# Front of a fused attention and gated-FFN kernel: eight value channels mixed without a copy, copies dealt out anew, and the first query products moved ahead of the mixing weights

## The chip, the cores and the metric

The kernel runs on one core of a Trainium2 chip. The time is the device time of one execution in microseconds (us), the median of several runs. Names used below: PE is TensorE's matrix products, PEld its weight loads, DVE is VectorE, ACT is ScalarE, POOL is GpSimd, SP is SyncE. PSUM is the memory that TensorE writes and that VectorE and ScalarE copy from.

## The reference, cut to what matters

Four batches, eight heads, a sequence of 768, head size 64, eight blocks of 96 positions. An 8 x 8 matrix `P` per batch and head is normalised five times by rows and columns, and mixes the blocks of k and v. Each block of q then attends to its mixed block, and the result goes through a gated FFN (512 to 1536 to 512).

```python
for _ in range(5):
    P = np.exp(P - np.max(P, axis=-1, keepdims=True))
    P = P / (np.sum(P, axis=-1, keepdims=True) + 1e-09)
    P = P / (np.sum(P, axis=-2, keepdims=True) + 1e-09)
k_sorted = np.einsum('bhij,bhjcd->bhicd', P, k_b)
v_sorted = np.einsum('bhij,bhjcd->bhicd', P, v_b)
scores = scale * np.matmul(q_b, k_sb.transpose(0, 1, 2, 4, 3))
attn = softmax(scores)                       # shortened
x = np.matmul(attn, v_sb)                    # heads put side by side: 3072 x 512
out = (silu(x @ w_gate) * (x @ w_val)) @ w_out
```

## The kernel before, in words

The order on each engine is written out by hand (`manual_schedule`): all engines for the front part (batch 0 up to the first FFN products), TensorE and GpSimd after it. The change is in the front.

**Loads.** GpSimd issues the loads in order: v of batch 0 in two halves of 48 positions (`load_v`), the first half of q (`load_q0(0)`), k of batch 0 in two halves, and, behind its own copies, the gate and value weights (`load_gv`), the second half of q, v of batch 1 and so on. A natural v tile `v_tiles[0]` has 64 partitions (head and block) by positions by 64 channels.

**Copies of v.** Mixing v needs, for each channel, the 96 positions side by side. `copy_v` writes v from position-major into `vch`, which is channel-major (64 channels of 96 positions). Before the change it is dealt out by positions: GpSimd copies positions 0 to 24 and 72 to 96, and channels 40 to 64 of positions 60 to 72 (lines 150 to 152); ScalarE copies 24 to 36 after the exponential of iteration 2, 36 to 48 after that of iteration 3 (lines 201 to 204), and 48 to 72 less GpSimd's part after the loop (lines 218, 219).

**Normalisation.** Five iterations go to and fro between ScalarE (exponential, line 196) and VectorE (lines 206 to 212), with a small result `p_bf` (line 215). Meanwhile TensorE runs products whose result nothing reads: `dots(124)`, then a few 512-column ones (`fill`) behind each iteration's row sums (lines 454 to 458).

**Mixing weights.** `weights(0)` and `weights(1)` (line 464) spread `p_bf` over the two halves of the partitions into the bank `w_ps`; `mix_rows` (line 469, VectorE) masks it into the mixing matrix `rmix[0]`, whose low rows serve v and both halves serve k.

**Chunks.** `v_chunk(b, at, n, eng, tag)` makes the mixed v of n channels, one product for each (line 276, tile `tv`): the channel's 96 positions (and 32 columns beyond, which are not read later) are the weights, 128 columns wide, and `rmix` is what is streamed. Then `drain` copies the chunk out of PSUM into `vt`, on VectorE ("v", line 223) or ScalarE ("s", line 225). `k0_chunk` (line 265, tile `tk`) and `q0_chunk` (line 255, tile `tq`) do the same for k and q into `kqt`, two products for each position. The tag names the PSUM room: "a" and "b" are one tile of two banks each, "gen" is three single banks in turn, "x" is one bank. A chunk of 16 takes "a" or "b", smaller ones a "gen" bank. The normalisation's `p_ps`, `w_ps` and the v and k chunks share "gen"; `w_ps` is read until the mixing matrices of batches 1 to 3 are made, after the chunks.

**The order on TensorE at the end of the front** (lines 472 to 490) is

```python
weights(0); weights(1)
mix_rows(low); mix_rows(high)
q0_chunk(0, 0, 16, "s", "b")
v_chunk(0, 0, 8, "v", "gen"); v_chunk(0, 8, 8, "s", "gen"); v_chunk(0, 16, 16, "v", "a")
v_chunk(0, 32, 8, "v", "gen"); v_chunk(0, 40, 16, "s", "b"); v_chunk(0, 56, 8, "s", "gen")
k0_chunk(0, 16, "v", "a"); k0_chunk(16, 16, "s", "b"); k0_chunk(32, 8, "v", "gen"); k0_chunk(40, 8, "s", "gen")
q0_chunk(0, 16, 8, "v", "a")
fill(idle_ps, 4)
qk(0, 0, "a"); qk(0, 1, "b")
```

(calls put on fewer lines, arguments of `mix_rows` shortened). `qk` are the first score products (line 308), which need all of `kqt`. After the scores, the products with v (`av`, line 335) and the transposes follow the FFN's products (lines 386, 404, 421), in which the attention of the later batches is spread out.

Of the kernel before, what the change touches and what calls it, by code (L numbers as in the profile page):

```python
# [10 lines left out]
BF16 = mybir.dt.bfloat16  # L11
# [6 lines left out]
def kernel(  # L18
# [11 lines left out]
    nc = tc.nc  # L30

    B, H, S, D = q.shape
    NB = sort_net.shape[-1]
    C = S // NB
# [21 lines left out]
    vnp = ctx.enter_context(tc.tile_pool(name="vnp", bufs=1))  # L56
# [18 lines left out]
    vch = const.tile([128, D * C + 32], BF16)  # L75
# [8 lines left out]
    v_tiles = {}  # L84
# [18 lines left out]

    def load_v(b, lo, hi):
        if b // 2 not in v_tiles:
            v_tiles[b // 2] = vnp.tile([128, C, D], BF16, name=f"v{b // 2}", tag="vn")
        u = b % 2
        nc.gpsimd.dma_start(out=v_tiles[b // 2][u * R:(u + 1) * R, lo:hi], in_=v_nat[b, :, lo:hi, :])

# [3 lines left out]
    def load_gv(lo, hi):  # L113
        load_w(wg_sb, wg_dram, lo, hi)
        load_w(wv_sb, wv_dram, lo, hi)

    def copy_v(eng, pair, rows, s, n=4, d0=0, d1=D):
        cs = slice(s * (C // n), (s + 1) * (C // n))
        dst = vch3[rows, d0:d1, cs]
        src = v_tiles[pair][rows, cs, d0:d1]  # L120
        if eng is nc.scalar:
            eng.copy(dst, src.transpose([0, 2, 1]))  # L122
        else:
            eng.tensor_copy(dst, src.transpose([0, 2, 1]))  # L124
# [8 lines left out]
    HC = C // 2  # L133
# [7 lines left out]
    def load_q0(t):  # L141
        nc.gpsimd.dma_start(out=q0[t].rearrange("p c d -> p (c d)"), in_=q_runs[0, t])

    load_v(0, 0, HC)
    load_v(0, HC, C)
    make_identity(nc, ident)
    load_q0(0)
    for a, rows in enumerate(halves):
        nc.gpsimd.dma_start(out=k0[rows], in_=k_nat[0, :, a * HC:(a + 1) * HC, :])
    copy_v(nc.gpsimd, 0, lowr, 0)  # L150
    copy_v(nc.gpsimd, 0, lowr, 3)
    copy_v(nc.gpsimd, 0, lowr, 5, 8, 40, D)
    load_gv(0, 512)
    load_q0(1)
    load_gv(512, 1024)
    load_gv(1024, DF)
    load_v(1, 0, HC)
    load_v(1, HC, C)
    for lo, hi in ((0, 64), (64, C)):
# [35 lines left out]
    for it in range(N_ITER):  # L195
        nc.scalar.activation(p_ps, p_sb if it == 0 else p_ps, AF.Exp)
        if it == 1:
            with nc.allow_low_precision("0/1 mask"):
                nc.vector.tensor_reduce(mask, id4, axis=AX.XY, op=ALU.add)
            nc.scalar.copy(sel, ident.rearrange("p (r g two) -> p two g r", g=H2, two=2))  # L200
        if it == 2:
            copy_v(nc.scalar, 0, lowr, 2, 8)
        if it == 3:
            copy_v(nc.scalar, 0, lowr, 3, 8)
        rowred = rowreds[it]
        nc.vector.reduce_sum(rowred[:, :, 0], p_ps, axis=AX.X)
        nc.vector.reciprocal(rowred, rowred)
        nc.vector.tensor_mul(p_ps, p_ps, rowred.to_broadcast([BH, NB, NB]))
        nc.vector.reduce_sum(colred[:, 0, :], p_ps.transpose([0, 2, 1]), axis=AX.X)
        nc.vector.reciprocal(colred, colred)  # L210
        if it < N_ITER - 1:
            nc.vector.tensor_mul(p_ps, p_ps, colred.to_broadcast([BH, NB, NB]))
    for lo in (0, NB // 2):
# [1 line left out]
        nc.vector.tensor_tensor(  # L215
            p_bf[:, part], p_ps[:, part].unsqueeze(2).to_broadcast([BH, NB // 2, H, NB]),
            colred.unsqueeze(1).to_broadcast([BH, NB // 2, H, NB]), op=ALU.mult)
    copy_v(nc.scalar, 0, lowr, 4, 8)
    copy_v(nc.scalar, 0, lowr, 5, 8, 0, 40)

    def drain(eng, dst, src):
        if eng == "v":
# [13 lines left out]
    def chunk_tile(name, n, tag):  # L236
        return pair_tile(name, tag) if n == 2 else bank_tile(name, tag)
# [12 lines left out]
    def q0_chunk(t, at, n, eng, tag):  # L250
        dst = kqt_tile(0)[:, GI * C:2 * GI * C].rearrange("p (g t r c) -> p t g r c", g=H2, t=2, c=QC)[:, t]
        tp = chunk_tile("tq0", n // 8, tag).rearrange("p (l g r) -> p l g r", l=n, g=H2)
        for lc in range(n):
            for two in range(2):
                nc.tensor.matmul(tp[two * D:(two + 1) * D, lc], lhsT=q0[t][:, at + lc, :],
                                 rhs=sel[:, two], start=True, stop=True)
        drain(eng, dst[:, :, :, at:at + n], tp.rearrange("p l g r -> p g r l"))

    def k0_chunk(at, n, eng, tag):
        dst = kqt_tile(0)[:, 0:GI * C].rearrange("p (n a c) -> p a n c", a=2, c=HC)  # L260
        rm = rmix[0].rearrange("p a (g two) i -> p two a g i", two=2)
        tp = chunk_tile("tk0", n // 8, tag).rearrange("p (l a n) -> p l a n", l=n, a=2)
        for lc in range(n):
            for two in range(2):
                nc.tensor.matmul(tp[two * D:(two + 1) * D, lc].rearrange("p a (g i) -> p a g i", g=H2),
                                 lhsT=k0[:, at + lc, :], rhs=rm[:, two], start=True, stop=True)
        drain(eng, dst[:, :, :, at:at + n], tp.rearrange("p l a n -> p a n l"))

    def v_chunk(b, at, n, eng, tag):
        rows = slice(0, 128) if b % 2 else lowr  # L270
        dst = vt_tile(b // 2)[:, b % 2]
        mix = rmix[b][rows, 0].rearrange("p a b -> p (a b)")
        tp = chunk_tile("tv", n // 8, tag).rearrange("p (l n) -> p l n", n=H * NB)
        for ld in range(n):
            col = (at + ld) * C
            nc.tensor.matmul(tp[:, ld, :], lhsT=vch[rows, col:col + 128], rhs=mix,  # L276
                             start=True, stop=True)
        drain(eng, dst[:, :, at:at + n], tp[0:C].transpose([0, 2, 1]))

    def v_pair_chunk(pair, at, n, eng, tag):  # L280
# [168 lines left out]
    def dots(n):  # L449
        for _ in range(n):  # L450
            nc.tensor.matmul(idle_ps[0:32, 0:32], lhsT=warm_sb[:, 0:32], rhs=warm_sb[:, 0:32],
                             start=True, stop=True)

    dots(124)
    for it, n in ((1, 3), (2, 4), (3, 4), (4, 4)):
        nc.tensor.matmul(idle_ps[0:NB, 0:NB], lhsT=rowreds[it][:, :, 0], rhs=rowreds[it][:, :, 0],
                         start=True, stop=True)
# [4 lines left out]
    def weights(half):  # L462
        for i in range(NB):
            nc.tensor.matmul(w_ps[halves[half], i].rearrange("p b h -> p (b h)"),
                             lhsT=p_bf[:, i].rearrange("p a b -> p (a b)"),
                             rhs=ident[0:BH, 0:BH], start=True, stop=True)

    def mix_rows(dst, rows, b):
        nc.vector.tensor_tensor(dst, mask[rows].unsqueeze(2).to_broadcast([R, H, NB]),
                                w_ps[rows, :, b].transpose([0, 2, 1]), op=ALU.mult)  # L470

    weights(0)
    weights(1)
    mix_rows(rmix[0][lowr, 0], lowr, 0)
    mix_rows(rmix[0][highr, 1], highr, 0)
    q0_chunk(0, 0, 16, "s", "b")
    v_chunk(0, 0, 8, "v", "gen")
    v_chunk(0, 8, 8, "s", "gen")
    v_chunk(0, 16, 16, "v", "a")
    v_chunk(0, 32, 8, "v", "gen")  # L480
# [1 line left out]
    v_chunk(0, 56, 8, "s", "gen")  # L482
    k0_chunk(0, 16, "v", "a")
    k0_chunk(16, 16, "s", "b")
    k0_chunk(32, 8, "v", "gen")
    k0_chunk(40, 8, "s", "gen")
    q0_chunk(0, 16, 8, "v", "a")
    fill(idle_ps, 4)
# [105 lines left out]
        return todo  # L594

    for s in range(4):
        copy_v(nc.gpsimd, 0, highr, s)
    load_k_pair()
    load_v(2, 0, C)
    load_v(3, 0, C)  # L600
# [8 lines left out]
    merge(ffn(1), kqs(1, (4.6, 5.9, 10.4)) + vs(v_chunk, 16, (7.2, 7.9, 8.5, 9.1))  # L609
          + units(1, range(4), (11.7, 16.4), (3.1, 2.4)))  # L610
    for s in range(4):
        copy_v(nc.gpsimd, 1, both, s)
    nc.vector.memset(kqt_tile("p")[:, 2 * GI * C:], 0.0)
    merge(ffn(2), units(1, range(4, 8), (0.0, 5.5)) + kqs("p", (13.0, 14.7, 20.7)) + v_pairs([(0, 22.5)])
          + [(13.0, lambda: q_dma(2)), (16.4, lambda: q_dma(3))])
# [40 lines left out]
```

## Time and profile before

| what | value |
|---|---|
| time before, median of 3 runs | 248.41 us (248.22 to 248.43) |
| the profiled execution's own time | 248.79 us |
| its span, first to last instruction | 246.7 us |
| PE busy | 236.6 us, 96% of the span |
| PEld, DVE, ACT, POOL busy | 140.3, 157.7, 109.8, 50.3 us |
| granted TensorE clock | 1.0 throughout |
| first value product (`tv`) | 12.65 us after the span's start |
| first score product (`qk`) | 18.41 us |
| first FFN product (`g_ps`) | 23.16 us |
| products of the FFN (lines 386, 404, 421), busy | 76.6, 77.3, 62.1 us |

Times in the views are microseconds from the span's start. Busy times of matrix products overlap one another, since they are pipelined; what counts for TensorE is the distance from start to start. The chain that ended last goes back from the last instruction to whatever released it, step by step: a line of it is a piece of the time.

### The profile page before, as it was taken

To read this page: it belongs to the slowest core of one execution; us is meant where nothing else is said; L and a number is where in the kernel's file an instruction comes from. 1 tells how busy PE (TensorE), PEld (TensorE's weight loads), DVE (VectorE), ACT (ScalarE), POOL (GpSimd) and SP (SyncE) were. 2 spreads that over 40 slices of the span, in tenths; PEclk is the share of its full clock that TensorE was granted. 3 is DMA by queue.
4 is the path that set the end of the run, shared out by engine and by line. 5 is a ranking of instruction groups with operands and counts; after the bars stand their busy time and mean duration, and the time that the engine had idled before them with its cause. 6 is when DMAs were issued, how large, how long until landed. Compare 5 with 4: busy or idle time off the path is not lost.

```text
span 246.7 us, 6160 instructions
## 1 busy us (share of the span) xinstructions
PE 236.6 (96%) x2609; PEld 140.3 (57%) x2633; DVE 157.7 (64%) x332; ACT 109.8 (45%) x186; POOL 50.3 (20%) x44
## 2 busy tenths in 40 slices
PE   6799999998999999999999999999999999999995
PEld 6375666575555566655555655565555555555543
DVE  6786779888455685867557746755764585446700
ACT  3977653364444444354642642254245334222311
POOL 5992139990098000000000000000000000000000
PEclk9999999999999999999999999999999999999999
DMA  5989999999999195110121111112111211100122
GB/s 96 215 121 208 206 220 210 203 224 222 183 183 161 40 201 127 45 45 0 45 74 35 58 58 35 44 43 78 32 43 45 50 48 53 43 27 20 43 82 88
DMA packets 36682, 24.38 MB, mean 99 GB/s; under 512 B 27696, under 2 KB 32560, under 8 KB 36272
## 3 DMA queue, kind: packets, MB, share of 16 engines
q0 software_dynamic: 18480, 14.16, 37.6%
q1 hardware_dynamic: 18176, 9.84, 14.2%
q8 instruction: 20, 0.33, 0.5%
q14 instruction: 6, 0.05, 0.1%
HBM read 28.32 MB, written 7.86 MB: 147 GB/s over the span
## 4 chain that ended last, share of the span: by engine, by line
PE 84%; DVE 7%; issue 3%; ACT 2%; DMA 2%; DVEq 0%; POOLq 0%
PE g_ps L386 24%; PE v_ps L404 24%; PE o_ps L421 23%; PE tkq L245 3%; PE qk L308 3%; PE av_ps L335 3%; DMA v<-in_v_dram 2%; DVE st L341 2%; DVE vt L223 1%; DVE gs_sb L396 1%; PE o_ps L437 1%; DVE h L409 1%; PE idle_ps L447 1%; PE tv L276 1%; PE x_ps L352 1%
## 5 line engine op out<-in xcount | busy, mean ns | idle before, releaser
L396 DVE SCALAR_TENSOR_TENSOR gs_sb<-th_sb,g_ps 128x384 bf16<-128x384 bf16 x96 | 52.9, 551 | 46.6 <-ACT th_sb L394 43.5
L404 PE MATMUL v_ps<-xt,wv_sb 128*128 128x384 bf16 x380 | 77.3, 326 | 0.1
L386 PE MATMUL g_ps<-xt,wg_sb 128*128 128x384 bf16 x376 | 76.6, 325 | 0.2
L394 ACT ACTIVATE th_sb<-g_ps 128x384 bf16<-128x384 f32 x96 | 47.2, 491 | 57.7 <-PE g_ps L386 55.1
L421 PE MATMUL o_ps<-wo,h 128*128 128x512 bf16 x255 | 62.1, 379 | 1.3 <-issue 0.3
L409 DVE SCALAR_TENSOR_TENSOR h<-v_ps,gs_sb 128x384 bf16<-128x384 f32 x96 | 53.3, 556 | 7.1
L404 PEld LDWEIGHTS <-wv_sb 128*128 128x128 bf16 x380 | 35.4, 97 | 23.9 <-issue 1.0
L386 PEld LDWEIGHTS <-wg_sb 128*128 128x128 bf16 x376 | 35.0, 97 | 24.3 <-issue 0.6
L421 PEld LDWEIGHTS <-h 128*128 128x128 bf16 x276 | 25.8, 98 | 27.9
L426 ACT COPY o_sb<-o_ps 128x512 f32<-128x512 f32 x23 | 13.5, 586 | 45.2 <-PE o_ps L421 45.2
L124 POOL COPY vch<-v 64x1536 bf16<-64x1536 bf16 (+2 forms) x11 | 28.7, 2639 | 14.1 <-DMA v<-in_v_dram 14.0
L321 ACT ACTIVATE e_all<-qk 96x768 bf16<-96x768 f32 x30 | 22.5, 802 | 8.4 <-PE qk L308 8.4
L341 DVE TENSOR_TENSOR st<-av_ps,r_sb 96x512 bf16<-96x512 f32 x32 | 21.7, 680 | 0.2
L335 PEld LDWEIGHTS <-e_all 96*128 96x128 bf16 x256 | 11.9, 98 | 4.9 <-ACT e_all L321 0.9
L339 DVE RECIPROCAL r_sb<-av_ps 96x8 f32<-96x8 f32 x32 | 6.4, 199 | 12.3 <-PE av_ps L335 12.2
L335 PE MATMUL av_ps<-vt,e_all 96*128 96x65 bf16 x256 | 13.1, 193 | 0.1
L223 DVE CAST vt<-tv 96x1024 bf16<-96x1024 f32 (+1 forms) x9 | 9.8, 1098 | 2.6 <-PE tv L286 1.7
L225 ACT CAST vt<-tv 96x1024 bf16<-96x1024 f32 (+1 forms) x9 | 8.1, 914 | 5.5 <-PE tv L286 3.6
L447 PE MATMUL idle_ps<-warm_sb 128*128 128x512 bf16 x22 | 6.1, 381 | 0.4 <-issue 0.2
L223 DVE COPY oh_sb<-o_ps 128x256 f32<-128x256 f32 x1 | 0.4, 425 | 9.3 <-PE o_ps L437 9.3
L371 POOL DMA_DIRECT2D q_scr<-in_q_dram x2 | 5.7, 3232 | 0.0
L122 ACT COPY vch<-v 64x768 bf16<-64x768 bf16 (+1 forms) x4 | 5.5, 1387 | 0.3 <-DMA v<-in_v_dram 0.3
(80 smaller groups left out, 133.1 us busy)
## 6 DMA issues: line engine op xcount, KB each, us to landing
out_dram<-o_sb SPq DMA_DIRECT2D x23, 256.0 KB, 2.0
v<-in_v_dram POOLq DMA_DIRECT2D x4, 384.0 KB, 12.7
wg_sb<-in_moe_w_gate_dram POOLq DMA_DIRECT2D x3, 512.0 KB, 11.3
wv_sb<-in_moe_w_val_dram POOLq DMA_DIRECT2D x3, 512.0 KB, 13.1
wo<-in_moe_w_out_dram POOLq DMA_DIRECT2D x3, 512.0 KB, 15.8
kp<-in_k_dram POOLq DMA_DIRECT2D x2, 768.0 KB, 10.0
v<-in_v_dram POOLq DMA_DIRECT2D x2, 768.0 KB, 16.5
q_scr<-in_q_dram POOLq DMA_DIRECT2D x2, 768.0 KB, 25.0
```

The costliest lines, as they stand in the source:

```text
L124: eng.tensor_copy(dst, src.transpose([0, 2, 1]))
L223: nc.vector.tensor_copy(dst, src)
L321: nc.scalar.activation(e_all[:, n:n + 2, 0:4 * C], wide[0:C, :, 0:4 * C], AF.Exp, scale=scale)
L335: nc.tensor.matmul(o[:, two, i4, 0:D + 1], lhsT=e[:, i4 * C:i4 * C + 128], rhs=vt[:, 2 * g + two, half * 4 + i4, 0:D + 1], start=True, sto ...
L341: nc.vector.tensor_tensor(st.rearrange("p i two d -> p two i d"), o[0:C, :, :, 0:D], r_sb.to_broadcast([C, 2, 4, D]), op=ALU.mult)
L386: nc.tensor.matmul(g_ps, lhsT=wg_sb[:, kc, ts(m, 128)], rhs=xt[:, kc, :], start=(kc == 0), stop=(kc == NKC - 1))
L394: nc.scalar.activation(th_sb, g_ps, AF.Tanh, scale=0.5)
L396: nc.vector.scalar_tensor_tensor(gs_sb, th_sb, 1.0, g_ps, op0=ALU.add, op1=ALU.mult)
L404: nc.tensor.matmul(v_ps, lhsT=wv_sb[:, kc, ts(m, 128)], rhs=xt[:, kc, :], start=(kc == 0), stop=(kc == NKC - 1))
L409: nc.vector.scalar_tensor_tensor(h_tiles[n][:, m, :], v_ps, 0.5, gs_tiles.pop(m), op0=ALU.mult, op1=ALU.mult)
L421: nc.tensor.matmul(o_ps, lhsT=h_w[:, m, ts(t3, 128)], rhs=wo_sb[part][:, m % 4, :], start=(m == 0), stop=(m == NFC - 1))
L426: nc.scalar.copy(o_sb, o_ps)
```

## The change

- **Direct channels.** The natural v tile gets 128 positions instead of 96. GpSimd fills positions 96 to 128 of its low 64 partitions with zeros (2,048 elements each). Channels 0 to 7 of batch 0 take their weights straight from it: 128 columns, 64 elements apart.
- **Copies.** Only channels 8 to 63 are copied. GpSimd takes positions 0 to 36 and 74 to 96; ScalarE 36 to 48 after the exponential of iteration 3 (nothing any more after that of iteration 2) and 48 to 74 after the loop. GpSimd fills the low rows of channels 0 to 7 of `vch` with zeros (768 elements), behind the issue of the weight loads.
- **Order.** The first query chunk stands ahead of `weights(0)`, right behind the four unread products; then `weights(0)`, the low mixing rows and the eight direct channels; `weights(1)` and the high rows come behind these.
- **Key chunk.** The chunk at 32 is cut in two of four positions, one for VectorE, one for ScalarE, each with a "gen" bank.
- **Unread products.** `dots(132)` for `dots(124)`.

```diff
-            v_tiles[b // 2] = vnp.tile([128, C, D], BF16, name=f"v{b // 2}", tag="vn")
+            v_tiles[b // 2] = vnp.tile([128, 128, D], BF16, name=f"v{b // 2}", tag="vn")
...
-    def copy_v(eng, pair, rows, s, n=4, d0=0, d1=D):
-        cs = slice(s * (C // n), (s + 1) * (C // n))
+    def copy_v(eng, pair, rows, c0, c1, d0=0, d1=D):
+        cs = slice(c0, c1)
...
+    nd = 8
+    v_tiles[0] = vnp.tile([128, 128, D], BF16, name="v0", tag="vn")
...
-    copy_v(nc.gpsimd, 0, lowr, 0)
-    copy_v(nc.gpsimd, 0, lowr, 3)
-    copy_v(nc.gpsimd, 0, lowr, 5, 8, 40, D)
+    nc.gpsimd.memset(v_tiles[0][lowr, C:], 0.0)
+    copy_v(nc.gpsimd, 0, lowr, 0, 36, nd, D)
+    copy_v(nc.gpsimd, 0, lowr, 74, C, nd, D)
...
     load_gv(1024, DF)
+    nc.gpsimd.memset(vch[lowr, 0:nd * C], 0.0)
     load_v(1, 0, HC)
...
-        if it == 2:
-            copy_v(nc.scalar, 0, lowr, 2, 8)
         if it == 3:
-            copy_v(nc.scalar, 0, lowr, 3, 8)
+            copy_v(nc.scalar, 0, lowr, 36, HC, nd, D)
...
-    copy_v(nc.scalar, 0, lowr, 4, 8)
-    copy_v(nc.scalar, 0, lowr, 5, 8, 0, 40)
+    copy_v(nc.scalar, 0, lowr, HC, 74, nd, D)
...
-        tp = chunk_tile("tk0", n // 8, tag).rearrange("p (l a n) -> p l a n", l=n, a=2)
+        tp = chunk_tile("tk0", n // 8, tag)[:, 0:n * 64].rearrange("p (l a n) -> p l a n", l=n, a=2)
...
-            nc.tensor.matmul(tp[:, ld, :], lhsT=vch[rows, col:col + 128], rhs=mix,
-                             start=True, stop=True)
+            direct = b == 0 and at + ld < nd
+            nc.tensor.matmul(tp[:, ld, :], lhsT=v_tiles[0][rows, :, at + ld] if direct else vch[rows, col:col + 128],
+                             rhs=mix, start=True, stop=True)
...
-    dots(124)
+    dots(132)
...
+    q0_chunk(0, 0, 16, "s", "b")
     weights(0)
+    mix_rows(rmix[0][lowr, 0], lowr, 0)
+    v_chunk(0, 0, 8, "v", "gen")
     weights(1)
-    mix_rows(rmix[0][lowr, 0], lowr, 0)
     mix_rows(rmix[0][highr, 1], highr, 0)
-    q0_chunk(0, 0, 16, "s", "b")
-    v_chunk(0, 0, 8, "v", "gen")
     v_chunk(0, 8, 8, "s", "gen")
...
-    k0_chunk(32, 8, "v", "gen")
+    k0_chunk(32, 4, "v", "gen")
+    k0_chunk(36, 4, "s", "gen")
     k0_chunk(40, 8, "s", "gen")
```

The calls of `copy_v` for the other rows are written in the new arguments and copy what they did.

More of the change, by code (lines that the diff above doesn't have):

```diff
@@ L596 @@
     for s in range(4):
-        copy_v(nc.gpsimd, 0, highr, s)
+        copy_v(nc.gpsimd, 0, highr, s * QC, (s + 1) * QC)
     load_k_pair()
@@ L611 @@
     for s in range(4):
-        copy_v(nc.gpsimd, 1, both, s)
+        copy_v(nc.gpsimd, 1, both, s * QC, (s + 1) * QC)
     nc.vector.memset(kqt_tile("p")[:, 2 * GI * C:], 0.0)
```

## The prediction

> **What bounds the kernel now.** I read the engine shares first, then the chain that ended last in order of time, then the timeline of the first 20 us engine by engine, and last the order of the changed kernel's instructions with their waits.
>
> ```profile
> PE 236.6 (96%) x2609; PEld 140.3 (57%) x2633; DVE 157.7 (64%) x332; ACT 109.8 (45%) x186; POOL 50.3 (20%) x44
> PEclk9999999999999999999999999999999999999999
> PE 84%; DVE 7%; issue 3%; ACT 2%; DMA 2%; DVEq 0%; POOLq 0%
> ```
>
> TensorE is busy for 96% of the span at full granted clock, so from about 25 us on the kernel is a queue of matrix products that nothing in the change touches. The change lives in the first 18.4 us, before the first score products (tile `qk`). There the chain hops between engines, and a shift of the first `qk` product passes one to one to the end: after 17 us the waits of TensorE name ScalarE, VectorE or issue, never a DMA or GpSimd. The piece that matters:
>
> ```profile
> 11.65 0.43 PE w_ps L464 x12
> 12.09 0.62 PE tq L255 x32
> 12.71 0.35 PE tv L276 x8
> 13.06 0.03 issue
> 13.09 0.69 DVE vt L223
> 13.77 0.01 issue
> 13.79 1.23 DVE vt L223
> 15.02 0.04 issue
> 15.06 0.71 PE tk L265 x32
> 15.77 0.02 issue
> 15.79 1.83 DVE kqt L223 x2
> 17.62 0.04 issue
> 17.67 0.81 PE idle_ps L447 x3
> 18.48 0.62 PE qk L308 x24
> ```
>
> Columns are start, length, what. After 13.1 us VectorE's copies out of PSUM carry the chain: the second `vt` copy (16 channels) frees the two-bank tile "a" at 15.02, the first key chunk uses it, and VectorE copies that chunk from 15.79. The later query chunk again needs "a", so it starts when that copy ends. Single instructions in this stretch: key copies start at 15.793 (1.224 long) and 16.934 (0.680 long); the query chunk's 16 products start from 17.069 to 17.315; the first `qk` starts at 18.412, the end of four unread products of 0.216 each plus 0.1 for a change of shape.
>
> The copies that the change deals out anew, and what else it leans on:
>
> ```profile
> L124 POOL COPY vch<-v 64x1536 bf16<-64x1536 bf16 x2 | 5.6, 2821 | 2.0 <-DMA v<-in_v_dram 2.0
> L122 ACT COPY vch<-v 64x768 bf16<-64x768 bf16 x3 | 4.5, 1512 | 0.3 <-DMA v<-in_v_dram 0.3
> L122 ACT COPY vch<-v 64x480 bf16<-64x480 bf16 x1 | 1.0, 1012 | 0.0
> 2.42 0.25 POOL masks.py:197 MEMSET ident<- 128x128 bf16 x1
> L276 PE MATMUL tv<-rmix,vch x128: 186/190/199, 12.6 to 57.3; 64*128 64x64 bf16 x64, 128*128 128x64 bf16 x64
> ```
>
> GpSimd's copies cost 1.72 ns per element plus 0.18 us (2.82 us for 1,536; 0.68 for 288), ScalarE's 1.68 to 1.76 ns plus about 0.2.
>
> **Part by part, in order of time.**
>
> *Normalisation.* The copy at iteration 2 (6.31 to 7.85 on ScalarE) goes. It held the fourth exponential until 7.756; its input was ready at 7.453, so it now starts at 7.49: 0.27 us earlier. The smaller copy of 12x56 = 672 elements (1.34 us) behind it ends near 8.97, before the fifth exponential at 9.17. The last row reduction, and with it the four unread products, move 0.27 us ahead: the last one starts at 10.67.
>
> *Query chunk ahead of the weights.* Its data lands at 10.61 (trace), so it is not late: 10.67 + 0.31 (unread product to another shape, as 18.101 to 18.412) = 10.98. Its 32 products take 0.50 between first and last start: 11.48. Then `weights(0)`: 11.59 to 11.81, end 12.00; the mixing row on VectorE 12.04 to 12.26; the first value product at 12.30 against 12.65 now. A lead of 0.35 us, but only for eight channels. Their copy out of PSUM moves from 13.09 to 12.73.
>
> *What stands behind them.* `weights(1)` (eight products, 0.03 apart) and two changes of shape at 0.12 each now lie between channel 7 and channel 8: 12.50 + 0.12 + 0.21 + 0.12 = 12.95, against 12.88 now. The lead is gone. The second mixing row, which ran in VectorE's idle time, now stands behind the first copy, but ends at 13.57 and delays nothing.
>
> *The copies.* Channel 8 needs all of them. ScalarE: 26x56 = 1,456 elements, 2.65 us from 9.42 (the second half of v lands at 9.37): 12.07, so ready. GpSimd: 2,016 elements (3.64) and 1,232 (2.30), 5.9 us against 6.3 now. But ahead of them stands a new fill of 2,048 zeros. No row has it; from the 128-element fill (0.25 us) and the one-element fills (0.10) it is 1.2 ns per element, 2.5 us, from 4.6 to 7.1, of which 1.7 lie in the present idle time. Bounds: at a constant 0.1 us it is hidden and the copies end at 12.3; at the copy's 1.72 ns it ends at 8.1 and they end at 14.0. I take the fill row, nearest in kind: copies end at 13.01, channel 8 starts at 13.05, 0.17 late. GpSimd's queue then holds the weight loads, which are issued about 0.15 us later; the second fill (768 zeros, about 0.9 us) delays only v's second batch, whose next issue already waits 0.5 us. First use of the gate weights (22.9 us, landed 18.65) has 4 us of cover.
>
> *Strided weight loads.* Now a value product starts every 0.029 us. No row of TensorE reads columns 128 bytes apart. Lower bound: the same 0.029. Upper: ScalarE's price for the same strided read, 1.76 ns x 128 = 0.225 us in each of the seven steps between the eight: +1.37 us, of which 0.10 hides behind the GpSimd copies. I take no loss, as the row is of the same instruction, and keep the upper end for the range. A loss of 0.029 each would cost 0.20, 0.10 of it on the path.
>
> [...]
>
> *Value and key chunks.* Channel 8 at 13.05 puts the 16-channel copy at 13.95 (now 13.79), the first key product at 15.21 (15.06), its copy at 15.94 (15.79): +0.15.
>
> *The new wait.* The key chunk at 32 is cut in two, giving VectorE 256 elements instead of 512 (0.41 for 0.68) and ScalarE the rest. But each half takes a bank "gen". There are three, and the mixing weights hold one. In the changed order the first product of the last chunk (at 40) waits for VectorE, where it waited for ScalarE, and the query chunk behind it has lost its own VectorE wait: the last chunk now waits for a small chunk's copy, which stands on VectorE behind the 1.22 us copy. So: 15.94 + 1.14 + 0.41 + 0.04 = 17.53 for the last key chunk, which was done by 16.98. Behind it on TensorE stand the query chunk (17.79 to 18.03, now 17.07 to 17.32), the unread products and `qk`. From the query chunk's last start to `qk` it is 1.10 now: 18.03 + 1.10 = 19.13. ScalarE's last key copy (to 18.59) and VectorE's last (to 18.94) are covered by the unread products.
>
> **Sum.** `qk` moves from 18.41 to 19.13, +0.7 us: 0.15 from copies and inserted weights, the rest from the bank. The eight more tiny products at the start fill idle time before 4.86. The profiled execution took 248.79 us (span 246.70, 2.09 around it), so it would take 249.5; the median of the runs shown is 248.41, 0.38 lower, so 249.1.
>
> **The rivals.**
> 1. *The bank is free in time.* If the last key chunk does not wait, the query chunk follows the "a" tile at +0.15 to +0.2 (+0.1 with the fill hidden): 248.5 to 248.6. Against it stand the wait in the order and the bank count.
> 2. *The front's lead carries through (not slower).* The lead of 0.35 us would have to survive `weights(1)`; its place is channel 8, and it decides if that starts before 12.88, with copies done by 12.8 and no bank wait. Even whole it gives 248.1. For it: the first products do start earlier. Against: two shape changes and eight products cost 0.45, more than the lead.
> 3. *Strided loads or the fill are dear.* From +0.1 to +1.3 (loads) or +1.0 (fill at the copy's price, channel 8 at 14.07 instead of 13.05) on top: 249.2 to 250.4.
>
> **How the numbers follow.** Forecast 0.57 (248.85 to 249.4), rival 3 0.22, rival 1 0.15, rival 2 and anything faster 0.06. The range 248.6 to 250.2 leaves out most of rival 2 and the top of rival 3. A measurement here tells 0.2%, 0.5 us: faster means below 247.9, which only a cause that I do not see would give (0.05); within it lie rivals 1 and 2 and the forecast's lower edge (0.18); the rest is slower (0.77).
>
> **What would show it.** Right: the first `tv` product near 12.3 reading `v`, channel 8 near 13.05, the last 16 `tk` products in a group of their own from 17.5 after a TensorE gap of about 1 us, `qk` near 19.1. Wrong: no gap ahead of them (rival 1), `tv` products over 0.03 us apart (rival 3), the zero fill ending before 6.3 or after 7.5, or a later stage that takes the 0.7 us back.

## The result and the profile after

The changed kernel takes 252.15 us (six runs, 251.25 to 253.34) where the kernel before took 248.42 beside it: 1.0145 times, with an interval from 1.0109 to 1.0181. The prediction was 249.1 with a range of 248.6 to 250.2, so the sign was right and the size far off: +3.7 us instead of +0.7. The profiled execution took 251.98 us, its span is 250.2. From the page of the changed kernel, the shares of the engines, the granted clock in 40 slices, and the gate group:

```profile
PE 239.7 (96%) x2641; PEld 142.2 (57%) x2641; DVE 157.5 (63%) x332; ACT 109.0 (44%) x185; POOL 52.4 (21%) x45
...
PEclk9979999999999999999999999999999999999999
...
L387 PE MATMUL g_ps<-xt,wg_sb 128*128 128x384 bf16 x376 | 76.6, 325 | 2.6 <-issue 2.4
```

Two things are new. The third digit of the clock is a 7: between 12.5 and 18.8 us TensorE did not have its full clock all the time (0.50 of it from 15.12 to 18.53). And the gate products, which are no part of the change, have 2.4 us of idle time in front of one of them, put down to "issue".

The chain in order of time (start, length, what) answers to the one shown of before:

```profile
3.00 8.24 DMA qk<-in_q_dram
...
11.28 0.69 PE tq L255 x32
...
12.63 0.82 PE tv L277 x8
13.45 0.35 PE w_ps L465 x8
13.80 0.82 PE tv L277 x24
...
14.64 1.23 DVE vt L223
...
15.92 1.08 PE tk L265 x32
...
17.02 1.57 DVE kqt L223 x2
...
18.62 0.44 PE tk L265 x16
```

In this execution the first query chunk waits for its data, so that the chain comes from the load of q and no longer over the normalisation. Then the mixing weights, eight direct channels, the second weights and the other channels follow each other, and the last 16 key products stand behind VectorE's second key copy. In the traces of the two kernels:

| first start of, us | before | after | moved by |
|---|---|---|---|
| `tv`, channel 0 | 12.65 | 12.63 | -0.02 |
| `tv`, channel 8 | 12.89 | 13.73 | +0.84 |
| `tk` | 15.06 | 15.92 | +0.86 |
| last 16 `tk` | 16.54 | 18.62 | +2.08 |
| `qk` | 18.41 | 20.22 | +1.81 |
| `g_ps` | 23.16 | 24.97 | +1.81 |
| `tkq` (second batches' keys) | 48.70 | 50.51 | +1.81 |
| last product of all | 243.37 | 246.81 | +3.44 |

So there are two losses. By the first score product it is 1.8 us. Then a pause of TensorE between 54 and 57 us brings the distance to 4.13 us (from the starts of the gate products), and at 60 us, where only the kernel before pauses, 0.7 us of it comes back: 1.6 us in all.

The pause of the changed kernel, by TensorE's own timeline (start, length, engine, line, operation; in brackets the idle time before it):

```profile
53.05 1.20 PE L245 MATMUL tkq<-rmix,kq 128*64 128x64 bf16 x64
56.62 0.81 PE L387 MATMUL g_ps<-xt,wg_sb 128*128 128x384 bf16 x4 [2.37 <-issue]
```

From 54.05, the start of the last `tkq` product, to 56.62 no product starts. The profile names no operand that is late. Before has a pause of this kind too, 0.72 us from start to start at 59.45, in the middle of a chunk:

```profile
60.17 0.44 PE L245 MATMUL tkq<-rmix,kq 128*64 128x64 bf16 x16 [0.52 <-issue]
```

The trace has a clue. A DMA queue named "instruction" (q8) moves 20 packets of 16,384 bytes in each of the two profiled executions. In the changed kernel one of them starts at 54.30, a quarter of a us into the pause, and the queue of GpSimd's loads is full in that stretch. The DMA view of 50 to 58 us, by queue:

```profile
q0 software_dynamic: 324, 1.78, 108.3%
q8 instruction: 1, 0.02, 0.8%
```

The loads in question are k and v of batches 2 and 3, issued by GpSimd from 47.8 us on, and a copy of q behind them. The idea for the experiments, a guess that no view states: TensorE waits for such a packet, as the next piece of its program, and the packet stands behind these loads.

### The profile page after: what moved, and what is told of

The parts are those of the page before. It is cut to its first block, busy times and chain, and to the rows that moved or that the text cites. A ratio compares the mean times of both kernels' runs of the same rounds, so it can differ in the third digit from the quotient of the medians.

```text
span 250.2 us, 6200 instructions
## 1 busy us (share of the span) xinstructions
PE 239.7 (96%) x2641; PEld 142.2 (57%) x2641; DVE 157.5 (63%) x332; ACT 109.0 (44%) x185; POOL 52.4 (21%) x45
## 4 chain that ended last, share of the span: by engine, by line
PE 84%; DVE 6%; DMA 3%; issue 3%; ACT 1%; POOL 1%; DVEq 0%; POOLq 0%
PE g_ps L387 23%; PE v_ps L405 23%; PE o_ps L422 23%; DMA qk<-in_q_dram 3%; PE tkq L245 3%; PE qk L309 3%; PE av_ps L336 3%; DVE st L342 2%; PE tv L277 1%; DVE gs_sb L397 1%; PE o_ps L438 1%; DVE vt L223 1%; DVE h L410 1%; PE x_ps L353 1%; PE tq L255 1%
## 5 line engine op out<-in xcount | busy, mean ns | idle before, releaser
L422 PE MATMUL o_ps<-wo,h 128*128 128x512 bf16 x276 | 64.7, 379 | 0.0
L124 POOL COPY vch<-v 64x1536 bf16<-64x1536 bf16 (+3 forms) x10 | 28.4, 2884 | 11.6 <-DMA v<-in_v_dram 11.5
L448 PE MATMUL idle_ps<-warm_sb 128*128 128x512 bf16 x25 | 6.9, 382 | 0.0
L309 PEld LDWEIGHTS <-kqt 64*128 64x128 bf16 x128 | 3.1, 94 | 3.5 <-issue 2.6
```

What stands on the lines that cost most here:

```text
L422: nc.tensor.matmul(o_ps, lhsT=h_w[:, m, ts(t3, 128)], rhs=wo_sb[part][:, m % 4, :], start=(m == 0), stop=(m == NFC - 1))
```

## The experiments

Three causes were on the table: the strided weight reads (rival 3 of the prediction), the halved clock, and the pause. Each kernel below is the kernel before (names with b_) or the changed one (a_, and u_ for those that keep only a part of the change) with the edit shown. Each time is compared with the kernel before as measured beside it (248.37 to 248.62 us).

### Being late, and eight more products

**b_late** delays the first score products by 1.7 us with products of the same number:

```diff
-    dots(124)
+    dots(116)
...
-    fill(idle_ps, 4)
+    fill(idle_ps, 12)
     qk(0, 0, "a")
```

> The kernel before, made late on purpose: 8 unread 32-column products fewer at the start, 8 unread 512-column ones more ahead of the first score product, so that TensorE's program has the same length and each later instruction its old place, but everything from the first score product on comes 8 x 0.216 = 1.73 us later, while GpSimd's loads stay where they were. Theory 1 (the 2.57 us gap of the changed kernel at 54 us is TensorE's program arriving late behind loads, because TensorE is late against them): a gap of 1 to 3 us between 45 and 65 us, total 248.4 + 1.7 + 1 to 2 = 251.1 to 252.1. Rival (the gap comes from where the 16 added instructions put the borders of the program's pieces): no new gap, 250.1. If lateness is taken back somewhere: below 250.

**b_dots** adds only the change's eight small products at the very start:

```diff
-    dots(124)
+    dots(132)
```

> The kernel before with 132 instead of 124 tiny unread products at the start, the only part of the change that alters the length of TensorE's program (16 instructions). Theory 1: these end before the first row-sum product, nothing is late, 248.4 +- 0.2. Rival (place of the program's pieces): the gap of about 2.5 us shows near 54 us, total near 250.

b_late: 251.21 us, ratio 1.011 (1.0087 to 1.0133). `qk` moved by 1.70, the last product by 2.56, and a pause of 1.39 us between two starts has come at 55.22, while the clock stayed full from 10.3 us on. What ended this pause is less plain than in the changed kernel:

```profile
56.61 0.63 PE L276 MATMUL tv<-rmix,vch 128*128 128x64 bf16 x16 [1.07 <-DVE gs_sb L396]
56.61 0.50 PEld L276 LDWEIGHTS <-vch 128*128 128x128 bf16 x15 [1.30 <-issue]
```

The product is put down to VectorE's `gs_sb`, which ended at 56.17, 0.44 us before it; the weight loads behind it, which wait for nothing that the profile shows, start at 56.61 as well. The prediction's "passes one to one to the end" is therefore wrong, also with nothing of the change in the kernel: 1.7 us late at 18 us cost 2.8 at the end.

b_dots: 249.15 us, ratio 1.0025 (1.0012 to 1.0038). Its front is where it was (`qk` 18.36), but the pause of 0.72 us is gone and another stands ahead of the gate products:

```profile
53.93 0.81 PE L386 MATMUL g_ps<-xt,wg_sb 128*128 128x384 bf16 x4 [1.55 <-issue]
```

Eight products more (sixteen instructions with their weight loads) in idle time cost 0.7 us 50 us later. The expectation of no change is missed. The author's reading is that they shift which instruction stands at the place where TensorE stops, and so when it is reached; the section on the hardware has the count behind it.

### Parts of the change taken out, with the pause left in

**a_whole** has the key chunk at 32 in one piece again:

```diff
-    k0_chunk(32, 4, "v", "gen")
-    k0_chunk(36, 4, "s", "gen")
+    k0_chunk(32, 8, "v", "gen")
```

> The changed kernel with the key chunk at 32 whole again on VectorE, so that the last key chunk takes a bank that ScalarE has freed. Theory 1 (bank wait costs 0.55 to 0.6 of the front's 1.81 us): no TensorE gap ahead of the last 16 key products, first score product 0.5 to 0.6 us earlier at about 19.6 to 19.7, total 0.5 lower or more if the later gap shrinks with the lateness. Rival (the bank wait hides behind the half clock or VectorE's chain): under 0.2 us earlier.

252.87 us, ratio 1.0163 (1.0125 to 1.0201): no faster. The wait is gone all the same; all 96 key products stand in one group, and from the first of them to `qk` it is 3.90 us instead of 4.30. The 0.40 us were lost again, as far as the profile shows: it has the pause (2.59 us at 53.20) and a second half-clock stretch behind it.

**a_contig** lets the eight direct products read 128 elements side by side from the same tile; these channels of batch 0 then hold other values (line shortened):

```diff
-  lhsT=v_tiles[0][rows, :, at + ld] if direct else ...
+  lhsT=v_tiles[0][rows, 2 * (at + ld):2 * (at + ld) + 2, :].rearrange("p c d -> p (c d)") if direct else ...
```

> The changed kernel with the eight direct products taking 128 elements side by side (two positions) of the same tile in place of one channel's strided column, so eight channels of batch 0 get other values; waits, sizes and order are the same. Theory 1 (strided weight loads cost 0.06 us each and, by keeping the array idle, help the clock drop): direct products 0.029 us apart instead of 0.082, the change to the mixing weights 0.12 instead of 0.18 us, first score product at least 0.45 us earlier; perhaps no half-clock window, then 0.8 earlier. Rival (the spacing is set by something else, such as data not ready): spacing stays near 0.08.

250.87 us (249.45 to 252.24), ratio 1.0091 (1.0066 to 1.0115). The products stand 0.029 us apart (12.23 to 12.43), strided 0.081 on average (12.63 to 13.20: the first step is 0.029, the others about 0.09). The weight loads of the changed kernel between 12 and 16 us (busy us, mean ns of one) show why:

```profile
L277 PEld LDWEIGHTS <-vch 64*128 64x128 bf16 x56 | 1.9, 100 | 0.0
L277 PEld LDWEIGHTS <-v 64*128 64x128 bf16 x8 | 0.9, 196 | 0.2 <-issue 0.2
```

Same shape, same type; the step between columns differs, and a load took 196 ns against 100. With the columns side by side, from the same tile `v`, the eight loads took 95 ns each in a_undo_contig. So the strided half of rival 3 is shown, at 0.052 us for each step on average. The time of the whole kernel is not explained by it: the profile still had the half clock (14.46 to 21.29) and a pause of 1.91, and `qk` came at 20.61, later than in the changed kernel and not the 0.45 us earlier that were expected.

**a_order** goes back to the old order of TensorE in the front:

```diff
+    weights(0)
+    weights(1)
+    mix_rows(rmix[0][lowr, 0], lowr, 0)
+    mix_rows(rmix[0][highr, 1], highr, 0)
     q0_chunk(0, 0, 16, "s", "b")
-    weights(0)
-    mix_rows(rmix[0][lowr, 0], lowr, 0)
     v_chunk(0, 0, 8, "v", "gen")
-    weights(1)
-    mix_rows(rmix[0][highr, 1], highr, 0)
```

> The changed kernel with the old order on TensorE: both halves of the mixing weights first, both mixing rows, then the query chunk, then the direct products. Theory 1 (the new order puts weights(1) and two changes of shape between channel 7 and channel 8, and takes the query products, which fill all rows of the array, out of the thin window): channel 8 starts at 12.9 to 13.2 instead of 13.73, the window before stands near 35%, the clock holds in some executions, first score product 0.5 us or more earlier. Rival (order is worth nothing, since copies out of PSUM set the pace): first score product within 0.2 us of 20.2.

250.99 us, ratio 1.0086 (1.0058 to 1.0113), 1.2 us better than the changed kernel. Channel 8 starts at 13.14, 0.59 earlier than with the new order, but `qk` at 20.05 only 0.17 earlier, within what the rival expected: a half-clock stretch (14.27 to 17.69) and the bank wait (0.48) remain. Of the 0.85 us between the two profiled executions, 0.64 is a pause of 1.93 instead of 2.57.

### The clock, and smaller loads

**a_fill** trades two of the first small products for two of 512 columns behind the first weights:

```diff
-    dots(132)
+    dots(130)
...
     weights(0)
+    fill(idle_ps, 2)
     mix_rows(rmix[0][lowr, 0], lowr, 0)
```

> The changed kernel with two unread 512-column products between the mixing weights and the direct products, where TensorE waits for VectorE, and two tiny unread products fewer at the start, so the program keeps its length. In the profiles so far every half-clock window follows a 3.41 us window in which the products filled 25% to 34% of the array's time (columns x rows x columns of weights), and none follows one with 35% or more; the changed kernel's window is at 25%. Theory 1 (the clock drops because the change thins out the products there): the two add 0.43 us, 12 points, to that window, so it stands at 37% or more and the clock holds in most executions; first score product 0.4 to 0.8 us earlier against the first query product, though the direct products start about 0.15 us later. Rival (the drop has to do with the phase of the windows alone): half-clock window at 14 to 18 us as before.

252.17 us, ratio 1.0143 (1.0083 to 1.0203): nothing gained. But the four runs differ by their mean granted clock: 251.38 and 251.44 us at 0.999, 252.90 at 0.993, 254.17 at 0.985. A stretch of 3.41 us at half clock takes 0.007 off the mean; so two runs of four kept the clock, where none of the changed kernel's six did, and about 1.5 us goes with each stretch in this kernel. That is no price of the clock alone: the profiled run has a stretch in the front and one right behind its pause (3.19 us from 54.13).

**a_small** and **b_small** cut the loads of k and v of batches 2 and 3 into thirds (4,096 bytes a packet instead of 12,288), in the changed kernel and in the one before:

```diff
-            nc.gpsimd.dma_start(out=kq_tiles["p"][u * R:(u + 1) * R], in_=k_nat[2 + u])
+            for lo in range(0, C, 32):
+                nc.gpsimd.dma_start(out=kq_tiles["p"][u * R:(u + 1) * R, lo:lo + 32], in_=k_nat[2 + u, :, lo:lo + 32, :])
...
-    load_v(2, 0, C)
-    load_v(3, 0, C)
+    for lo in range(0, C, 32):
+        load_v(2, lo, lo + 32)
+    for lo in range(0, C, 32):
+        load_v(3, lo, lo + 32)
```

> The changed kernel with the k and v loads of batches 2 and 3 (packets of 12,288 bytes, about 0.9 us each, from 50.5 to 65 us) in three parts each, so packets of 4,096 bytes. Theory 1 (the gap at 54 us is a piece of TensorE's program, 16,384 bytes, queueing behind these packets on a DMA engine): the gap of 2.57 us shrinks to under 1.3 us, no half-clock window follows it, total 1 to 2 us lower than 252.15. Rival (the wait is for something that does not depend on packet size, such as the share of the DMA engines being at its limit): gap over 2 us.

> The kernel before with the same loads in three parts each. Theory 1: its gap of 0.72 us at 59 us goes or shrinks, total 0.2 to 0.7 us below 248.4, so a version that beats both. Rival: more load instructions and smaller packets cost as much, 248.4 or more.

a_small: 251.49 us, ratio 1.0102 (1.0044 to 1.016), pause 1.86 us. b_small: 248.39, ratio 0.9989 (0.9972 to 1.0006), its pause of 0.72 gone and the median the same. Inconclusive: with smaller packets the pause is shorter, but it lies between the under 1.3 us of the theory and the over 2 us of its rival.

### What remains of the change when only the direct channels and the copies are kept

**a_undo** has the old order, the whole key chunk and 124 first products (the edits of a_order and a_whole and the reverse of b_dots together); **a_undo_contig** is the same with a_contig's line, so with other values in eight channels.

```diff
-    dots(132)
+    dots(124)
...
-    q0_chunk(0, 0, 16, "s", "b")
     weights(0)
-    mix_rows(rmix[0][lowr, 0], lowr, 0)
-    v_chunk(0, 0, 8, "v", "gen")
     weights(1)
+    mix_rows(rmix[0][lowr, 0], lowr, 0)
     mix_rows(rmix[0][highr, 1], highr, 0)
+    q0_chunk(0, 0, 16, "s", "b")
+    v_chunk(0, 0, 8, "v", "gen")
...
-    k0_chunk(32, 4, "v", "gen")
-    k0_chunk(36, 4, "s", "gen")
+    k0_chunk(32, 8, "v", "gen")
```

> The changed kernel with the old order on TensorE, the key chunk at 32 whole and 124 tiny products again: what is left of the change are the eight direct channels and the copies dealt out anew. Theory 1: first value product 0.25 to 0.35 us earlier than before, channel 8 no earlier because of the strided loads (0.082 us apart), first score product within 0.3 us of 18.4 where the clock holds and about 1 us later where a half-clock window falls on it; total 248.5 to 249.8. Rival (the loss lies mainly with the direct channels and copies): above 250.5.

> The same with the direct products taking 128 elements side by side, so those eight channels get other values: what the direct channels and the new deal of copies would be worth if a strided load cost nothing. Theory 1: first score product 0.2 to 0.4 us earlier than before's 18.41, total 0.2 to 0.7 us lower than a_undo and at or below 248.4. Rival (GpSimd's copies hold channel 8 back): no better than before.

a_undo: 249.67 us, ratio 1.0055 (1.0038 to 1.0072). a_undo_contig: 247.73, ratio 0.998 (0.9967 to 0.9992), the first one ahead of before. The columns seem to cost 1.9 us, more than their products can by themselves: channel 8 starts at 13.40 in the one and 12.60 in the other, `qk` at 18.93 and 18.13. That left open how much of the 1.9 is the pause, so the pause had to go.

### The loads moved out of the way

**a_quiet** and **b_quiet** put 22 fills of an unused tile on GpSimd ahead of the issue of these loads, which then comes 12.8 and 13.2 us later:

```diff
+    junk = const.tile([128, 512], BF16)
+    for _ in range(22):
+        nc.gpsimd.memset(junk, 0.0)
     load_k_pair()
     load_v(2, 0, C)
```

> The changed kernel with 22 small fills of an unused tile on GpSimd ahead of the k and v loads of batches 2 and 3 (about 10 us of work), so that these loads start near 58 us instead of 48 and the DMA engines are idle when TensorE's program is fetched near 53. Theory 1 (the gap is that fetch queueing behind these loads): the gap of 2.57 us at 54 us is gone or under 0.4 us, total 1 to 2 us lower than 252.15, near 250.5; perhaps a smaller gap later. Rival (something else stops TensorE there): gap stays over 1.5 us.

> The kernel before with the same fills. Theory 1: its gap of 0.72 us at 59 us goes, total 0.3 to 0.7 us below 248.4, a version that beats both kernels; if another piece of the program now meets the loads later, nothing is won. Rival: the later loads make later stages wait, above 248.6.

a_quiet: 249.52 us, ratio 1.0059 (1.0035 to 1.0084), 2.6 us below the changed kernel. TensorE's timeline at the place of the pause, and the load queue of the same 50 to 58 us:

```profile
54.18 1.20 PE L245 MATMUL tkq<-rmix,kq 128*64 128x64 bf16 x64
55.31 0.82 PE L387 MATMUL g_ps<-xt,wg_sb 128*128 128x384 bf16 x4
```

```profile
q0 software_dynamic: 156, 0.14, 11.0%
```

TensorE's program is the same, the queue of loads has 11.0% of the engines' time instead of 108.3%, and the gate products follow without a break. b_quiet: nine of ten runs at 247.68 to 247.93, the tenth at 251.05, so its interval (0.9963 to 1.0018) takes in 1. The last four kernels repeat it and close the sum.

**u_quiet** and **u_quiet_contig** are a_undo and a_undo_contig with the 22 fills, **b_quiet_again** is b_quiet once more, and **a_quiet_fill** is a_quiet with four of the first small products traded for four of 512 columns behind `weights(0)` (a_fill's edit with 128 and 4):

```diff
-    dots(132)
+    dots(128)
...
     weights(0)
+    fill(idle_ps, 4)
     mix_rows(rmix[0][lowr, 0], lowr, 0)
```

> The version that keeps only the direct strided channels and the new copies (old order, whole key chunk, 124 dots; 249.67), with the 22 small fills that hold back the later loads. Theory (what is lost over the front's own delay is the code piece queued behind loads): the delay of qk now passes one to one; qk near 18.9, i.e. 0.5 behind the quiet version of before (247.74), so 248.2 to 248.4, and no TensorE gap over 0.6 us between 50 and 65 us. Rival (strided reads cost something of their own later, or the clock): stays at 249.2 or more.

> The same with the eight direct products of batch 0 reading 128 contiguous elements of the same tile (other values in these eight channels). Theory: qk near 18.1, 0.3 ahead of the quiet version of before, so 247.4 to 247.5; together with the strided one this prices the strided columns at 0.8 with the loads out of the way, against 1.9 with them in it. Rival (the 1.9 belongs to the columns themselves): 246.4, or no difference from its noisier sister at 247.7 and the strided one at 249.6.

> The kernel before with the 22 small fills ahead of the issue of the later key loads, a second time: 247.74 of ten runs the first time, with an interval that took in 1. Theory: 247.7 again in nearly all runs, 0.25% under the kernel before. Rival (a chance of that chip or that hour): 248.2 to 248.4.

> The changed kernel with the 22 small fills, and with four of the 132 first unread products replaced by four of 512 columns behind the first weights, in the stretch where the array was least used before the clock halved (25% of its area in 3.41 us; about 45% with these). They delay the first value product by about 0.45 us. Theory (the low use is what halves the clock): full clock in all runs, qk near 20.2 to 20.4 where it was 21.2, time 248.9 to 249.7. Rival (the clock falls for another reason): one or two half-clock stretches of 3.41 us as before, and 249.9 to 251.2.

| kernel | us | ratio to before (interval) |
|---|---|---|
| b_quiet_again | 247.91 | 0.9977 (0.9968 to 0.9987) |
| u_quiet_contig | 247.48 | 0.9959 (0.9947 to 0.9971) |
| u_quiet | 248.16 | 0.9989 (0.9977 to 1.0002) |
| a_quiet_fill | 250.16 | 1.0066 (1.0052 to 1.0079) |

b_quiet_again confirms that the kernel before gains as well when the loads come later, 0.56 us; its profile has no pause at 60 us, and it is the version that beats both. With the loads out of the way the strided columns cost 248.16 - 247.48 = 0.68 us, a third of the 1.9 that they cost with them. u_quiet's twelve runs also split by the clock: eight at 0.998 or more took 247.88 to 248.29, four at 0.992 or 0.993 took 248.55 to 248.91, about 0.65 us for a half-clock stretch. TensorE's timeline of the profiled executions, u_quiet first, shows both (channels 8 to 63, key products, score products; the first view ends at 19.6 us):

```profile
13.24 2.44 PE L277 MATMUL tv<-rmix,vch 64*128 64x64 bf16 x56
15.61 2.69 PE L265 MATMUL tk<-rmix,qk 128*64 128x64 bf16 x96
19.46 0.34 PE L309 MATMUL qk<-kqt 64*128 64x96 bf16 x7
```

```profile
12.71 2.03 PE L277 MATMUL tv<-rmix,vch 64*128 64x64 bf16 x56
14.88 1.94 PE L265 MATMUL tk<-rmix,qk 128*64 128x64 bf16 x96
18.23 0.68 PE L309 MATMUL qk<-kqt 64*128 64x96 bf16 x24
```

Channel 8 is 0.53 apart. Then the strided version's clock is halved from 14.65 to 18.07 and its 96 key products take 2.69 us instead of 1.94; `qk` is 1.23 apart, and these two executions took 248.87 and 247.60: 1.27. Without the pause, lateness did pass one to one here. a_quiet and b_quiet show it too: their profiled executions are 2.76 us apart at `qk` and 2.82 in time.

a_quiet_fill missed what the theory said of it. The fills stand ahead of the stretch in front of the half clock: full clock is on record from 5.86 here and from 4.97 in a_quiet, and the half clock lay that much later. This doesn't follow the number of small products: with 132 of them the record of full clock starts between 4.03 and 7.12 us, with 124 between 4.40 and 10.30. By stretch (start:end, length, busy time of PE, PEld, DVE, ACT, POOL with counts, then the clock, DMA share, GB/s):

```profile
12.68:16.10 3.42, 3.23 (x74) 2.91 (x73) 2.00 (x3) 1.18 (x3) 3.42 (x6) 1.00 0.71 81
16.10:19.51 3.41, 2.86 (x101) 2.72 (x102) 2.29 (x4) 2.37 (x4) 3.08 (x5) 0.50 1.24 203
```

The four fills start from 11.95 to 12.60, ahead of the first row; the thin products fill it, and the second row is at half clock. So this run neither priced the clock nor showed the fills' use; it does show that the stretch ahead of the half clock again held the thin products.

## Why the prediction was wrong, and where it was right

**Normalisation: right.** With the copy at iteration 2 gone, the last unread products run from 9.87 to 10.91; the forecast had the last one start at 10.67, it did at about 10.5.

**Query chunk: 0.3 late in this execution.** "Its data lands at 10.61, so it is not late" read one landing time that the kernel before covers with 1.4 us. In the profiled run of the changed kernel it landed at 11.24, and the waits name it:

```profile
PE tq L255 <- DMA qk<-in_q_dram: 0.4, 1, 0.4
PE tk L265 <- DVE kqt L223: 0.4, 1, 0.4
```

(waited for, total us, times, longest). The chunk started at 11.28, not 10.98, and the first channel at 12.63, not 12.30. With that the whole lead of the front was gone before the direct channels began. In the six other profiled kernels with this order (a_whole, a_contig, a_fill, a_small, a_quiet, a_quiet_fill) the chunk started at 10.83 to 11.00 without this wait, as forecast: the forecast was fair, and what it lacked was a margin for the load.

**What stands behind them: right, and the copies were no limit.** The 0.65 us from the first channel to channel 8 were worked out as two changes of shape, eight products and the eight channels, and these do stand in between: the second weights start at 13.38, channel 8 at 13.73. GpSimd's part, start, length:

```profile
4.57 1.85 POOL L152 MEMSET v<- 64x2048 bf16 x1
6.32 5.95 POOL L124 COPY vch<-v 64x2016 bf16<-64x2016 bf16 x2
```

The copies took the 5.9 us worked out; the zero fill took 1.85 us where 2.5 were taken (0.9 ns per element instead of 1.2), so the copies ended at 12.27 instead of 13.01 and delayed nothing.

**Strided weight loads: the term was taken at zero and measured 0.37 us in the front.** Seven steps of 0.081 on average instead of 0.029. "As the row is of the same instruction" was the wrong choice: a row of the same instruction with another step between its columns is not a row of this case, and ScalarE's copy with the same strided read was the nearer one (1.51 us for 768 elements, against 0.80 for its exponential of 768). The measured size lies nearer the lower end of the bounds (0.052 of at most 0.196 a step). From the first channel to channel 8 it was 1.10 us (forecast 0.65), and channel 8 came at 13.73 instead of 13.05. That strided columns cost nothing did not hold here: 196 ns for a strided load against 100 for a packed one. What in the load takes the time, no run shows.

**The new wait: right in kind, a little smaller.** The last 16 key products do stand in a group of their own behind VectorE's second key copy (0.4 us in the waits); taking the cut out gave 0.40 us in a_whole, where the forecast had about 0.55.

**The clock: not in the prediction at all.** From 15.12 to 18.53 TensorE had half its clock, and the key products stood 0.053 us a pair apart instead of 0.032. From the first key product to `qk` it is 4.30 us against 3.35 before: 0.40 of the 0.95 is the bank, the rest the clock. Without the bank wait this stretch is 3.85 us at half clock (u_quiet) and 3.35 at full clock (u_quiet_contig). The page of before has a row of nines and gave no sign of it.

**"A shift of the first qk passes one to one to the end": wrong, and the largest error.** It left out the pause behind 50 us. The pause of before stood in its waits (0.5 us in front of a `tkq` product, put down to "issue"), and the prediction read such a wait as no obstacle. b_late broke the step with nothing of the change in it, and the quiet kernels restored it. The sum, from the medians:

| part | from | us |
|---|---|---|
| whole | after - before, 252.15 - 248.42 | 3.73 |
| front alone | a_quiet - b_quiet, 249.52 - 247.74 | 1.78 |
| pause | the difference | 1.95 |
| of the front: strided columns | u_quiet - u_quiet_contig | 0.68 |
| of the front: order, cut chunk, eight products | a_quiet and u_quiet, each against its before: 1.15 + 0.31 | 1.46 |
| of the front: the copies, with direct channels made free | u_quiet_contig - b_quiet_again | -0.43 |

The last three, measured at two times, add up to 1.71. The front's 1.78 is what the trace shows at `qk` (1.81), and the pause's 1.95 is near the 1.63 that the last product lost after `qk`. It is not the bare pause: three of the changed kernel's six runs have a granted clock of 0.985 and took 252.32 to 253.34 us, the three at 0.993 took 251.25 to 251.98, and in a_whole and a_fill the second half-clock stretch begins right behind the pause. In the profiled execution the prediction's front would have been +0.7; with the query data (0.3), the columns (0.37) and the clock (0.55, from the 0.95 above) and less 0.15 of the bank it is 1.8. These terms don't stand apart from each other: in a_small, without the wait for the query data, the key products began 0.38 us earlier and `qk` only 0.08, as there the products right ahead of `qk` ran at half clock too (until 19.45).

**The rivals.** Rival 3 had one true half, the loads; the fill was cheap. Rival 1 fell (the wait is there), rival 2 too (channel 8 was late). None reached beyond 25 us.

**What stays open.** That TensorE stops for a piece of program code behind loads is the author's reading. The runs show that moving the loads removes the stop (2.57 us in the changed kernel, none there in a_quiet) and where the stops stand in TensorE's program (last section). As each stop ended 2.3 to 3.0 us after a packet of the queue "instruction" started, a packet that starts later against TensorE would make a longer one, by the same reading: in the changed kernel it started at 54.30, 0.24 us after the last product ahead of the stop, in a_quiet the answering one at 51.95, some 235 of TensorE's products and weight loads ahead of that place. What makes it start later among the loads is not shown. The clock's price in the changed kernel itself isn't settled: in a_quiet, by the mean clock, one run at full clock took 249.52, four with one half stretch 249.20 to 249.55, and two with two of them 250.75 and 251.18. Of the 1.46 us, the order, the cut chunk and the clock are not parted further.

## What to carry to other kernels

Before a delay is said to pass one to one, look at what keeps its own time farther on: here TensorE, late at 18 us, stopped for 1.39 us at 55 us, among the loads that GpSimd issues from about 48 us on, and 1.7 us late became 2.8 (b_late). A shift of instruction count alone, in idle time, cost 0.7 us in b_dots, as much as the prediction gave the whole edit, so this edit is best judged with those loads moved away, as in b_quiet, which is also the cheapest gain found (0.23%, b_quiet_again). A copy that an operand's strided read replaces wasn't free here (196 ns a load against 100): price the read by a row with the same step. And where a change leaves only thin products together, read the granted clock: a half-clock stretch cost about 0.65 us in u_quiet.

## What the hardware showed that was not expected

**The clock fell while TensorE was busy.** Here are, in the changed kernel, the stretch of 3.41 us ahead of the half clock and the one at half clock, and then the stretch of before that answers to the first (columns as in a_quiet_fill's table):

```profile
11.70:15.12 3.42, 3.12 (x89) 3.07 (x84) 1.60 (x4) 1.72 (x3) 3.42 (x6) 1.00 0.64 98
15.12:18.53 3.41, 3.01 (x95) 2.84 (x92) 2.85 (x4) 2.15 (x3) 3.37 (x5) 0.50 1.22 201
```

```profile
11.93:15.35 3.42, 3.20 (x121) 3.02 (x119) 2.69 (x5) 2.19 (x4) 3.42 (x6) 1.00 0.51 62
```

PE is busy for 91% of 11.70 to 15.12 after and for 94% of 11.93 to 15.35 before, yet the one is followed by half the clock and the other by the full one (the page of before has only nines). The two differ in how many products they hold (89 and 121) and in how large these are, which an estimate puts into one number: each product's streamed columns at 0.216/512 us (unread products of 512 columns start 0.216 us apart), times its weights' share of 128 x 128 (the largest in these kernels), summed over the stretch. It gives 25% after and 45% before; over the profiled runs, 25 to 36% for the stretches ahead of a half clock that began in the front (nine kernels) and 36% or more for those that kept it. In these nine profiles the half clock began 10.24 us, three such stretches, after the first record of full clock, and ended after one or two. That is a reading of these runs, not a test, and what halves the clock is not shown: the two ranges touch, and in the profiles of both attempts to raise this share (a_fill, a_quiet_fill) the stretch ahead of the half clock missed the added products. Where the stretches lie changed from profile to profile (full clock is on record from 4.03 us at the earliest, from 10.30 at the latest), so an edit could not be aimed at one. No wait of TensorE's products between 11 and 20 us is longer than 0.37 us in the changed kernel.

**TensorE stopped at the same places of its program.** The queue "instruction" has 20 packets of 16,384 bytes in the profile of before and in that of the changed kernel. The 18 profiles have 12 pauses of over 0.6 us from start to start behind 21 us, in eleven kernels. Each ended 2.3 to 3.0 us after such a packet started (2.33 in the changed kernel, 2.34 before). By a count of the recorded products and weight loads of TensorE, ten of them ended behind 1,719 to 1,725 (1,723 in the changed kernel), wherever that fell between 53 and 58 us, and the two near 60 us (before and a_undo_contig) behind 1,976. a_undo_contig has one of each kind, with 256 between them; 16,384 bytes over 256 would be 64 for each, an estimate that no run tests. The quiet kernels passed the same places without such a pause.

**A weight load from columns 128 bytes apart took 196 ns**, one of the same shape from packed columns 100 (changed kernel), and on average it was 0.081 against 0.029 us from product to product (0.094 in a_undo).
